# Reordering the first stages of a fused attention and FFN kernel, and 2x2 blocking for half of its last tile

## The chip, the cores and the metric

The kernel runs on one NeuronCore of a Trainium2 chip, in one launch. The metric is device time in microseconds. The five engines that the text speaks of are TensorE (PE, with its weight loads as PEld), VectorE (DVE), ScalarE (ACT), GpSimd (POOL) and SyncE (SP). Each works through its own list of instructions in order and waits at semaphores for the others. Inputs and the output lie in device memory as float32; the kernel computes in bfloat16 with float32 sums.

## The reference

Eight batches of cosFormer attention (8 heads, 576 positions, 64 features per head) feed a multiplicative feed-forward net. Cut to what matters:

```
theta = pi/2 * pos / 576
phi(x) = concat(relu(x)*cos(theta), relu(x)*sin(theta))     # 128 features
kv  = sum over s of phi(k)[s, f] * v[s, d];  z = sum over s of phi(k)
num = phi(q) @ kv;  den = phi(q) @ z + 1e-6
x   = num / den, heads side by side                          # 4608 x 512
a, b = x @ w1, x @ w2                                        # 512 -> 1024
out = ((a * b) @ w3) @ w_out                                 # 1024 -> 1024 -> 512
```

## The kernel before, in words

Attention is done per batch `b` in five chunks `c` of 128 rows (the last of 64). The net is done per tile `t` of 512 tokens, nine tiles in all, so that tile 0 holds rows of batch 0 alone and tile 1 begins with the last 64 rows of batch 0. `w3 @ w_out` is multiplied once into `w34b` (1024 x 512), and every tile then does `(a*b) @ w34b`.

The order of all work is written out by hand in the string `PLAN`; nothing reorders it, and each engine receives its instructions in the order in which the plan's steps issue them. A line of the plan starts with one step `f t` (or `w`, below), which advances tile `t` by one group of matmuls; the other steps of the line come behind it. The steps that the change touches:

- `idle n`: n matmuls of zeros, 128x512, whose result nobody reads (`idle_mms`, L454; tile `unread`).
- `q b c`, `k b c`: the features of a chunk, `x*cos` on DVE (L495) and `x*sin` on ACT (L499) or on DVE (L502). `v b c on`: a copy of `v` into the tile with the column of ones.
- `qt b c on`: eight PE transposes of the q features into the PSUM tile `pst` (two buffers), and a copy into `qpT` by DVE (`V`) or ACT (`A`) (`q_tr`, L567 and L573).
- `kv b`: 40 matmuls (L549) into `pnum`, then the copy `kvs` by ACT (L553) and DVE (L554). For batch 0 this is `kv0`, `ks0`, `kvs0`.
- `n b c`: eight matmuls of a q chunk with `kvs` (L581) into `pnum`. There is one such PSUM tile of two banks in this part of the kernel, so each `n` waits until the last one has been read. For `n 0 0` there is a tile of its own, `pfirst`.
- `d b c`: the division on DVE in three instructions (L592, L593, L594), which reads that PSUM tile and writes `xblk`.
- `xt b c on`: four transposes of `xblk` (L621) and a copy into the tile's `xT` by ACT or DVE (L622).
- `w12`, `wo`, `w3`, `l b name part`: loads, all issued by POOL, in order. A load of `w_out` (`wo a l0 n`) or `w3` (`w3 a g0 n`) covers 32 of the 128 partitions, so four of them make a half of `w_out` or two row blocks of `w3`. `l b k 0` and `l b k 1` are the two parts of a batch's k.
- `t3 jp`: DVE transposes row block `jp` of `w3` into the tile `w3T` (L464), of which there are `NT3` buffers. `w jp lc0 n`: n matmuls (L474) of that block with rows of `w_out`; after the last, ACT copies the sum into `w34b` (L477).
- `open` gives the four PSUM banks of the first part (`ps_first`) to the net's matmuls (`ffn_tile`, four buffers).

In a tile, `f` first makes `a` and `b` (L668): ACT copies `a` out of PSUM and DVE multiplies it with `b` (L711 and L718, L728 and L734, for tiles 0 and 1 also L692 and L694). In tiles 0 and 1 the first groups are cut into quarters of 128 tokens, so that the matmuls of the first 128 tokens can start with one chunk in `xT`. Then comes the product with `w34b`. Tiles 2 to 7 (`SEVEN`) do it as seven products of 256-row blocks with sums and differences on DVE (`seven_products`, `sums`, `weight_block`, L814 and L822). Tiles 0, 1 and 8 do it plainly: for each 128 tokens `ms`, eight matmuls of 512 columns (L749), a copy by ACT (L755) and a store. In tile 8 the last 128 tokens are cut into two halves of 256 columns (L766, L768).

Of the kernel before, what the change touches and what calls it, by code (L numbers as in the profile page):

```python
# [16 lines left out]
P = 128  # L17
# [9 lines left out]
q 0 1; idle 1; idle 1; q 0 0 4; idle 1; idle 1; qt 0 1 V; k 0 4; k 0 1 0; qs 0 3; k 0 0 0; k 0 2; idle 1; k 0 3; qt 0 0 A; ks0 4; idle 3; qc 0 3; ks0 1; kv0 4 0; q 0 2; kv0 1 0; ks0 0; kv0 2 0; kv0 4 1; ks0 3; kv0 0 0; ks0 2; kv0 0 1; kv0 3 0; kvs0 0 A; kv0 1 1; kv0 2 1; kv0 3 1; kvs0 1 V; qt 0 2 A; n0 0; n0 1; idle 1; idle 1; idle 1; w12 0 0 2; w12 1 0 2; w12 0 2 2; n 0 1; idle 2; w12 1 2 2; w12 0 4 2; d 0 0; w12 1 4 2; w12 0 6 2; w12 1 6 2; idle 1; wo 0 0 4; d 0 1; xt 0 0 A; wo 1 0 4; wo 2 0 4; wo 3 0 4; w3 0 0 2; w3 1 0 2; w3 2 0 2; w3 3 0 2; wo 0 4 4; wo 1 4 4; idle 1; qt 0 3 V; wo 2 4 4; wo 3 4 4; w3 0 2 2; w3 1 2 2; w3 2 2 2; w3 3 2 2; w3 0 4 2; w3 1 4 2; w3 2 4 2; w3 3 4 2; q04; w3 0 6 2; xt 0 1 V; w3 1 6 2; open; w3 2 6 2; n 0 2; w3 3 6 2; l 1 q 0; l 1 q 1; l 1 k 0  # L27
f 0; l 1 k 1
f 0; d 0 2; l 1 v 0
f 0; n 0 3; d 0 3; xt 0 2 A  # L30
# [22 lines left out]
w 4 4 4  # L53
# [49 lines left out]
f 2; xd 2 4; xd 3 1  # L103
# [159 lines left out]
NKP, NVA, NQP, NRQ, NRV, NT3 = 1, 2, 1, 2, 2, 3  # L263
# [51 lines left out]
def kernel(  # L315
# [135 lines left out]
    unread = ps_first.tile([P, 512], FP32, name="unread")  # L451
    kva = ps_first.tile([P, 512], FP32, name="kva")

    def idle_mms(n):  # L454

        for _ in range(n):
            nc.tensor.matmul(unread[:, :], lhsT=zeros[:, 0:128], rhs=zeros[:], start=True, stop=True)
# [105 lines left out]
    def q_tr(b, c, on):  # L563
        R = ROWS[c]
        pst = ps_tr.tile([P, 8, 128], BF16, name="pst")
        for h in range(H):
            nc.tensor.transpose(pst[:, h, :], att[b]["qp"][:, c, h, :], identb[:])  # L567
        cols = ds(columns_of(b, c), R)
        if on == "both":
            nc.scalar.copy(out=att[b]["qpT"][:, 0:4, cols], in_=pst[:, 0:4, 0:R])  # L570
            nc.vector.tensor_copy(out=att[b]["qpT"][:, 4:8, cols], in_=pst[:, 4:8, 0:R])
        else:
            on(out=att[b]["qpT"][:, :, cols], in_=pst[:, :, 0:R])  # L573
# [85 lines left out]
    def ffn_groups(t):  # L659
# [39 lines left out]
        seven = t in SEVEN  # L699
        s = [fsb.tile([P, 4, 256], BF16, name=f"s{i}", bufs=1) for i in range(3)] if seven else None  # L700
# [23 lines left out]
        for jc in range(4 if t <= 1 or t in BY_HALF else 0, 8):  # L724
            aT = ffn_tile()
            products(aT[:, :], w1b, jc, slice(0, 512))
            asb = fsb.tile([P, 512], BF16, name="asb")
            nc.scalar.copy(out=asb[:], in_=aT[:, :])  # L728
            newest[0] = asb
            yield  # L730
            bT = ffn_tile()
            products(bT[:, :], w2b, jc, slice(0, 512))
            abT = abT or new_abT()
            nc.vector.tensor_mul(out=abT[:, jc, :], in0=asb[:], in1=bT[:, :])  # L734
# [11 lines left out]
        for ms in range(3 if t == NT - 1 else 4):  # L746
# [14 lines left out]
        if t == NT - 1:  # L761
# [10 lines left out]


# [121 lines left out]
    def num_first(*half):  # L895

        t = att[0]["n"].get(0)
        if t is None:
            t = ps_first.tile([P, 2, 512], FP32, name="pfirst")
        num(0, 0, t, range(4 * half[0], 4 * half[0] + 4) if half else range(H))  # L900
# [3 lines left out]

    V, A, G = nc.vector.tensor_copy, nc.scalar.copy, nc.gpsimd.tensor_copy
# [38 lines left out]
    def store_behind_transposes():  # L944
# [11 lines left out]
        "qt": q_tr, "qh": q_tr_halves, "qd": q_dma, "kv": kv, "kv0": lambda c, *half: kv_first(c, False, *half), "ks0": lambda c: kv_first(c, True), "kvs0": kvs_first,  # L956
# [40 lines left out]
```

## Time and profile before

| | us |
|---|---|
| median of 3 runs (lowest, highest) | 244.58 (243.73, 245.21) |
| the profiled execution | 242.91 |
| its span, from the first to the last instruction | 241.1 |
| PE busy in the span | 234.6 |
| PE busy in the stretch 32 to 48 us | 15.31 of 16.00 |
| PE busy in the stretch 48 to 60 us | 12.00 of 12.00 |
| DVE busy in the stretch 32 to 48 us | 12.95 of 16.00 |
| DMA in the stretch 48 to 60 us | 199 GB/s |

The span leaves out 1.8 us of the execution. In the lists of instructions in order of time a row has the start, the length, the engine, the line, the operation, what it writes and reads with its shape, and how many instructions were merged into it; a bracket at the end tells how long the engine had been idle and whose event ended that. The matmuls of PE overlap: four of 512 columns take 0.86 us from the first start to the next group's start, although the row says 1.03.

### The profile page before, as it was taken

What the parts mean: (1) busy time and instruction counts of PE and PEld (TensorE: products, weight loads), DVE (VectorE), ACT (ScalarE), POOL (GpSimd) and SP (SyncE); (2) the same over time, 40 slices, a digit from 0 to 9 for tenths busy, and PEclk for the clock granted to TensorE, in tenths of its full rate; (3) what the DMA queues carried; (4) which work ended last, traced back from release to release, by engine and by line L of the source; (5) the groups of instructions that cost most, each with busy time, mean ns of one, the idle gap of its engine ahead of it and who ended that gap; (6) DMA issues with size and microseconds to landing.
All of it is one profiled execution on the core that took longest, in us unless ns stands there. A gap on an engine that the chain in (4) does not pass through costs nothing.

```text
span 241.1 us, 5777 instructions
## 1 busy us (share of the span) xinstructions
PE 234.6 (97%) x2227; PEld 162.5 (67%) x2227; DVE 191.9 (80%) x456; ACT 111.9 (46%) x198; POOL 80.0 (33%) x151
## 2 busy tenths in 40 slices
PE   8799989999999999999999999999999999999994
PEld 3589534476964595788579848875995798484442
DVE  6986569968988947999899989999999788786320
ACT  2833321687755832735475437437064312312321
POOL 8744888551803034105402405031020050272000
PEclk9999999999999999999999999999999999999999
DMA  7999999999999999979998987999756936599843
GB/s 200 191 196 199 186 171 186 199 198 197 185 179 137 151 133 182 194 115 163 164 172 105 208 113 107 155 143 136 100 195 129 127 74 157 118 305 312 243 158 130
DMA packets 84939, 40.48 MB, mean 168 GB/s; under 512 B 48048, under 2 KB 82096, under 8 KB 84912
## 3 DMA queue, kind: packets, MB, share of 16 engines
q0 software_dynamic: 37616, 23.60, 65.5%
q1 hardware_dynamic: 47296, 16.52, 39.2%
q8 instruction: 17, 0.28, 0.5%
q14 instruction: 10, 0.08, 0.1%
HBM read 38.80 MB, written 9.44 MB: 200 GB/s over the span
## 4 chain that ended last, share of the span: by engine, by line
PE 84%; DMA 10%; POOL 4%; issue 1%; DVE 1%; DVEq 0%; POOLq 0%
PE ffnps L668 46%; PE ffnps L814 14%; PE ffnps L749 8%; DMA w2b<-in_moe_w_dram 5%; PE ffnps L474 4%; PE pnum L581 4%; PE pnum L549 4%; DMA kf<-in_k_dram 3%; DMA early<-in_moe_w_dram 2%; PE ffnmore L814 1%; PE pst L567 1%; POOL early L407 1%; POOL early L413 1%; PE ffnps L766 1%; POOL w2b L922 1%
## 5 line engine op out<-in xcount | busy, mean ns | idle before, releaser
L668 PE MATMUL ffnps<-xT,w1b 128*128 128x256 bf16 (+2 forms) x448 | 76.3, 303 | 0.0
L668 PE MATMUL ffnps<-xT,w2b 128*128 128x256 bf16 (+2 forms) x448 | 76.2, 303 | 0.0
L668 PEld LDWEIGHTS <-w2b 128*128 128x128 bf16 x448 | 40.7, 98 | 19.6 <-issue 0.2
L668 PEld LDWEIGHTS <-w1b 128*128 128x128 bf16 x448 | 41.0, 98 | 18.8 <-issue 0.4
L728 ACT CAST asb<-ffnps 128x512 bf16<-128x512 f32 x40 | 23.4, 585 | 42.8 <-PE ffnps L668 38.3
L734 DVE TENSOR_TENSOR abT<-asb,ffnps 128x512 bf16<-128x512 bf16 x40 | 27.2, 682 | 14.9 <-PE ffnps L668 14.7
L711 ACT CAST asb<-ffnps 128x512 bf16<-128x512 f32 x24 | 14.1, 586 | 35.6 <-PE ffnps L668 28.5
L594 DVE TENSOR_TENSOR xblk<-pnum,den 128x512 bf16<-128x512 f32 (+1 forms) x39 | 26.9, 691 | 1.3
L499 ACT ACTIVATE kp<-kf,sinv 128x512 bf16<-128x512 bf16 (+4 forms) x33 | 21.0, 662 | 0.9 <-DMA kf<-in_k_dram 0.9
L749 PE MATMUL ffnps<-w34b,abT 128*128 128x512 bf16 x88 | 20.8, 379 | 0.0
L814 PEld LDWEIGHTS <-abT 128*128 128x128 bf16 x192 | 18.5, 98 | 3.1
L718 DVE TENSOR_TENSOR abT<-asb,ffnps 128x512 bf16<-128x512 bf16 x24 | 16.3, 687 | 5.1 <-PE ffnps L668 5.1
L419 POOL COPY seen<-xT 128x1 bf16<-128x1 bf16 x6 | 1.3, 210 | 57.3 <-DMA xT<-xblk 57.3
L499 ACT ACTIVATE qp<-qs,sinv 128x512 bf16<-128x512 bf16 (+6 forms) x30 | 18.1, 626 | 0.9 <-DMA qs<-in_q_dram 0.9
L581 PEld LDWEIGHTS <-qpT 128*128 128x128 bf16 x320 | 15.0, 98 | 4.4 <-DVE qpT L573 0.5
L581 PE MATMUL pnum<-kvs,qpT 128*128 128x65 bf16 x312 | 16.1, 194 | 0.0
L419 POOL COPY seen<-asb 128x1 bf16<-128x1 bf16 x14 | 3.0, 211 | 37.4 <-ACT asb L711 34.8
L474 PE MATMUL ffnps<-early,w3T 128*128 128x512 bf16 x64 | 14.5, 379 | 0.7 <-DVE w3T L464 0.7
L814 PEld LDWEIGHTS <-s 128*128 128x128 bf16 x144 | 14.0, 98 | 1.7
L495 DVE TENSOR_SCALAR kp<-kf,cosv 128x512 bf16<-128x512 bf16 (+1 forms) x40 | 14.8, 392 | 0.1
L749 PEld LDWEIGHTS <-abT 128*128 128x128 bf16 x88 | 8.1, 98 | 8.5
L376 POOL DMA_DIRECT2D vs<-in_v_dram x16 | 12.0, 766 | 2.5 <-DMA kf<-in_k_dram 1.5
(129 smaller groups left out, 341.0 us busy)
## 6 DMA issues: line engine op xcount, KB each, us to landing
out_dram<-osb SPq DMA_DIRECT2D x9, 256.0 KB, 3.4
kf<-in_k_dram POOLq DMA_DIRECT2D x7, 320.0 KB, 6.8
early<-in_moe_w_dram POOLq DMA_DIRECT2D x16, 128.0 KB, 5.1
qs<-in_q_dram POOLq DMA_DIRECT2D x6, 320.0 KB, 6.7
vs<-in_v_dram POOLq DMA_DIRECT2D x6, 320.0 KB, 7.9
kf<-in_k_dram POOLq DMA_DIRECT2D x7, 256.0 KB, 7.1
qs<-in_q_dram POOLq DMA_DIRECT2D x6, 256.0 KB, 7.3
vs<-in_v_dram POOLq DMA_DIRECT2D x6, 256.0 KB, 9.6
```

The source lines that it names most:

```text
L474: nc.tensor.matmul(acc[:, :], lhsT=w3T[:, lc, :], rhs=woutb[:, lc, :], start=(lc == 0), stop=(lc == 7))
L495: nc.vector.tensor_scalar(out=dst[:R, c, :, 0:D], in0=rows[:R], scalar1=0.0, scalar2=cosv[:R, at:at + 1], op0=ALU.max, op1=ALU.mult)
L499: nc.scalar.activation(out=dst[:R, c, 0:n, D:F], in_=rows[:R, 0:n], func=ACTF.Relu, scale=sinv[:R, at:at + 1], bias=0.0)
L581: nc.tensor.matmul(nt[:, h // 4, ds((h % 4) * 65, 65)], lhsT=qpT[:, h, ds(at, 128)], rhs=kvs[:, h, :], start=True, stop=True)
L594: nc.vector.tensor_tensor(out=xblk[rows, g0:g0 + ng], in0=n4[:, :, :, 0:D], in1=den[rows, 0:ng].unsqueeze(3).to_broadcast([R, ng, 4, D]), ...
L668: nc.tensor.matmul(out, lhsT=w[:, kc, ts(jc, 128)], rhs=x[:, kc, tok], start=(kc == 0), stop=(kc == 3))
L711: nc.scalar.copy(out=asb[:], in_=aT[:, :])
L718: nc.vector.tensor_mul(out=abT[:, ts(pair, 2), ts(half, 256)], in0=asb[:].rearrange("p (i n) -> p i n", i=2), in1=bT[:, :].rearrange("p (i ...
L728: nc.scalar.copy(out=asb[:], in_=aT[:, :])
L734: nc.vector.tensor_mul(out=abT[:, jc, :], in0=asb[:], in1=bT[:, :])
L749: nc.tensor.matmul(ops[:, :], lhsT=abT[:, jc, ts(ms, 128)], rhs=w34b[:, jc, :], start=(jc == 0), stop=(jc == 7))
L814: nc.tensor.matmul(into[:, ts(ms, 256)], lhsT=a[:, kc, ts(ms, 128)], rhs=b[:, kc, :], start=(ms == 0 and kc == 0), stop=(ms == 1 and kc == 3))
```

## The change

It has two parts. The first is in the plan, up to tile 1:

- four of the seven `idle` matmuls between the first `n` and the first `f 0` go, and three stay. In their place stand `qt 0 3`, copied by halves (the new step `qy`: half 0 by ACT, half 1 by DVE), and the matmuls of `n 0 2`, which write a new PSUM tile `spare` (step `ns`). `spare` takes the place of `unread` and `kva`: its first bank is the target of `idle` and of `ns`, its second is `kva`. Two of the three `idle` write `pfirst`.
- `f 0` starts before `xt 0 1`; `xt 0 1` and `n 0 3` follow its first group, and `d 0 2` and `d 0 3` come ahead of tile 0's first products on DVE.
- POOL loads `w3` row blocks 2 and 3 ahead of the second half of `w_out`. `w` runs the first four row blocks by halves: `w 0 0 4` to `w 3 0 4`, then `w 0 4 4` to `w 3 4 4`; `t3 2`, `t3 3`, `t3 4` and `t3 6` are done by halves, and `w3T` has four buffers.
- `kv 1` moves behind the next group of `f 0`. `k 2 4` and `k 2 2`, which stood behind `d 1 4`, now stand ahead of it; between `n 1 4` and `n 1 0` there is one group of `f 0` where there were two.
- `xd 3 1` and `xd 2 4` change places.

The second part is in tile 8: its first 256 tokens go through seven products of blocks of 128 rows and 256 columns (`small_products`), the sums of the left blocks being made by DVE in the loop over `jc`, the sums of the results by DVE and POOL. The last 256 tokens are done as before.

```
-... n0 0; n0 1; idle 1; idle 1; idle 1; w12 ...; n 0 1; idle 2; w12 ...; d 0 0; w12 ...; idle 1; wo 0 0 4; d 0 1; xt 0 0 A; wo 1 0 4; wo 2 0 4; wo 3 0 4; w3 0 0 2; w3 1 0 2; w3 2 0 2; w3 3 0 2; wo 0 4 4; wo 1 4 4; idle 1; qt 0 3 V; wo 2 4 4; wo 3 4 4; w3 0 2 2; w3 1 2 2; w3 2 2 2; w3 3 2 2; w3 0 4 2; ... q04; w3 0 6 2; xt 0 1 V; w3 1 6 2; open; w3 2 6 2; n 0 2; w3 3 6 2; l 1 q 0; l 1 q 1; l 1 k 0
-f 0; l 1 k 1
-f 0; d 0 2; l 1 v 0
-f 0; n 0 3; d 0 3; xt 0 2 A
+... n0 0; n0 1; qt 0 3 N; w12 ...; n 0 1; idle 1; ns 0 2; w12 ...; d 0 0; w12 ...; wo 0 0 4; d 0 1; qy 0 3 0 A; xt 0 0 A; wo 1 0 4; wo 2 0 4; wo 3 0 4; w3 0 0 2; w3 1 0 2; w3 2 0 2; w3 3 0 2; w3 0 2 2; w3 1 2 2; w3 2 2 2; w3 3 2 2; wo 0 4 4; wo 1 4 4; idle1 2; qy 0 3 1 V; d 0 2; wo 2 4 4; wo 3 4 4; w3 0 4 2; ... q04; w3 0 6 2; w3 1 6 2; open; w3 2 6 2; w3 3 6 2; l 1 q 0; l 1 q 1; l 1 k 0
+f 0; xt 0 1 A; n 0 3; l 1 k 1
+f 0; d 0 3; l 1 v 0
+f 0; xt 0 2 A
...
-f 0; lg 2 q 0; t3 1; l 2 k 0; l 2 k 1; l 2 q 1; t3 2; l 2 v 0
+f 0; lg 2 q 0; t3 1; l 2 k 0; l 2 k 1; l 2 q 1; l 2 v 0
 f 0
-f 0
+f 0; t3 2 0 4; t3 3 0 4; t3 2 4 4; t3 3 4 4
 w 0 0 4
-w 0 4 4
 w 1 0 4
-w 1 4 4
-w 2 0 4; t3 3; t3 4
-w 2 4 4; q 0 4 0
+w 2 0 4
 w 3 0 4
-w 3 4 4; t3 5; qt 0 4 V; t3 6
-w 4 0 4; n 0 4; t3 7; d 0 4
-w 4 4 4
+w 0 4 4; t3 4 0 4; t3 4 4 4
+w 1 4 4; q 0 4 0
+w 2 4 4
+w 3 4 4; t3 5
+w 4 0 4; qt 0 4 V; t3 6 0 4; t3 6 4 4
+w 4 4 4; n 0 4; t3 7; d 0 4
...
 f 0; qt 1 4 A; qt 1 2 A; l 3 q 0; v 2 2 G; v 1 0 V; v 1 1 V
-f 0; qt 1 0 A; v 1 2 V; v 1 3 V; kv 1
-f 0; qt 1 1 A; n 1 4; d 1 4; k 2 4; k 2 2 2
-f 0
+f 0; qt 1 0 A; v 1 2 V; v 1 3 V
+f 0; kv 1; qt 1 1 A; k 2 4; k 2 2 2
+f 0; n 1 4; d 1 4
 f 0; n 1 0; d 1 0; xt 1 4 A; q 2 0 0; q 2 1; lt 3 v 0; xt 0 4 A
...
-NKP, NVA, NQP, NRQ, NRV, NT3 = 1, 2, 1, 2, 2, 3
+NKP, NVA, NQP, NRQ, NRV, NT3 = 1, 2, 1, 2, 2, 4
...
-    unread = ps_first.tile([P, 512], FP32, name="unread")
-    kva = ps_first.tile([P, 512], FP32, name="kva")
+    pfirst = ps_first.tile([P, 2, 512], FP32, name="pfirst")
+    spare = ps_first.tile([P, 2, 512], FP32, name="spare")
+    kva = spare[:, 1, :]
...
-        seven = t in SEVEN
+        seven, small = t in SEVEN, t == NT - 1
...
-        for ms in range(3 if t == NT - 1 else 4):
+        if small:
+            yield from small_products(t, abT, s)
+        for ms in (2,) if small else range(4):
...
+    def small_products(t, abT, s):
+
+        s3, s2, s4 = (x[:, :, 0:128] for x in s)
+        t1, t2, t3, t4 = blocks
+        osb = osb_of(2 * t)
+        c11, c12, c21, c22 = (osb[:, r, ts(c, 256)] for r in range(2) for c in range(2))
+        a11, a12, a21, a22 = (A_small(abT, r, c) for r in range(2) for c in range(2))
+        b11, b21, b22 = B_of(0, 0), B_of(1, 0), B_of(1, 1)
...
+            for kc in range(4):
+                nc.tensor.matmul(bank[:, 0:256], lhsT=a[:, kc, :], rhs=b[:, kc, :], start=(kc == 0), stop=(kc == 3))
...
+        nc.scalar.copy(out=c11, in_=product(a11, b11))
+        nc.scalar.copy(out=c22, in_=product(s3, t3, True))
+        yield
+        m2 = product(a12, b21)
+        add(c21, product(s2, t2), c11)
+        yield
+        add(c12, product(a21, t1, True), c21)
+        add(c21, c21, c22, nc.gpsimd)
+        add(c11, m2, c11)
+        add(c22, c22, c12, nc.gpsimd)
+        yield
+        add(c21, product(a22, t4), c21)
+        store(nc.sync, osb[:, 1:2, :], 4 * t + 1, 1)
+        add(c12, product(s4, b22), c12)
+        store(nc.sync, osb[:, 0:1, :], 4 * t, 1)
+        yield
```

More of the change, by code (lines that the diff above doesn't have):

```diff
@@ L567, in q_tr, with q_copy @@
             nc.tensor.transpose(pst[:, h, :], att[b]["qp"][:, c, h, :], identb[:])
[L568 to L571, printed above, removed]
-        else:
-            on(out=att[b]["qpT"][:, :, cols], in_=pst[:, :, 0:R])
+        if on is None:
+            uncopied[b, c] = pst
+        else:
+            on(out=att[b]["qpT"][:, :, ds(columns_of(b, c), R)], in_=pst[:, :, 0:R])
+    uncopied = {}
+    def q_copy(b, c, half, on):
+        on(out=att[b]["qpT"][:, ts(half, 4), ds(columns_of(b, c), ROWS[c])],
+           in_=uncopied[b, c][:, ts(half, 4), 0:ROWS[c]])
     def num(b, c, tile=None, heads=range(H)):
@@ L895, in num_first @@
     def num_first(*half):
[L897 to L900, printed above, removed]
+        num(0, 0, pfirst, range(4 * half[0], 4 * half[0] + 4) if half else range(H))
     def kvs_first(i, on):
         on(out=att[0]["kvs"][:, 4 * i:4 * i + 4, :], in_=att[0]["halves"][i][:, 0:260])
+    N = None
     V, A, G = nc.vector.tensor_copy, nc.scalar.copy, nc.gpsimd.tensor_copy
```

47 lines of the change are left out of this document (29 added, 18 removed).

## The prediction

> **What bounds the kernel now.** I read first the page's head and the table of busy time by stretches, to see which engine has no idle time.
>
> ```profile
> span 241.1 us, 5777 instructions
> PE 234.6 (97%) x2227; PEld 162.5 (67%) x2227; DVE 191.9 (80%) x456; ACT 111.9 (46%) x198; POOL 80.0 (33%) x151
> ...
> 32.00:48.00 16.00, 15.31 (x83) 6.85 (x82) 12.95 (x25) 6.13 (x12) 11.94 (x20) 1.00 1.41 188
> 48.00:60.00 12.00, 12.00 (x165) 8.37 (x163) 9.00 (x29) 9.60 (x18) 3.92 (x4) 1.00 1.44 199
> 60.00:205.00 145.00, 144.98 (x1480) 109.58 (x1477) 129.82 (x314) 71.98 (x132) 34.62 (x70) 1.00 1.03 147
> ```
>
> Each row gives a stretch, its length, the busy time of PE, PEld, DVE, ACT and POOL, the granted clock, the DMA share and GB/s. From 60 to 205 us PE is busy for 144.98 of 145 us, at the full clock (1.00). So a microsecond that PE loses before 60 us is lost at the end too, and one that it gains arrives only if nothing on the way holds PE back. Next I read PE, DVE and ACT in order of time for the stretches that the diff touches. At the start:
>
> ```profile
> 13.81 0.81 PE L457 MATMUL unread<-zeros 128*128 128x512 bf16 x3
> 14.72 0.81 PE L457 MATMUL unread<-zeros 128*128 128x512 bf16 x3
> 15.59 0.38 PE L457 MATMUL unread<-zeros 128*128 128x512 bf16 x1
> 16.90 0.39 PE L668 MATMUL ffnps<-xT,w1b 128*128 128x128 bf16 x4
> 19.17 1.04 PE L668 MATMUL ffnps<-xT,w1b 128*128 128x256 bf16 x8
> ...
> 15.48 0.69 DVE L594 TENSOR_TENSOR xblk<-pnum,den 128x512 bf16<-128x512 f32 x1
> 17.06 0.41 DVE L622 COPY xT<-pst 128x512 bf16<-128x512 bf16 x1
> 17.39 0.15 DVE L592 TENSOR_SCALAR den<-pnum 128x8 f32<-128x8 f32 x1
> 17.82 0.69 DVE L594 TENSOR_TENSOR xblk<-pnum,den 128x512 bf16<-128x512 f32 x1
> ...
> 60.06 0.45 PE pst L567 x8
> 55.24 0.26 PE pnum L581 x8
> ```
>
> Seven zero products fill PE while DVE divides; the last two rows, of the chain that ended last, price eight transposes and eight matmuls of `n`. A division takes from 17.39 to 18.51, 1.12 us; `d 0 1` ends at 16.17. Then the stage of `w34b`:
>
> ```profile
> 31.80 3.62 PE L474 MATMUL ffnps<-early,w3T 128*128 128x512 bf16 x16
> 36.11 3.63 PE L474 MATMUL ffnps<-early,w3T 128*128 128x512 bf16 x16 [0.69 <-DVE w3T L464]
> ...
> 34.81 1.25 DVE L464 STREAM_TRANSPOSE w3T<-early 128x1024 bf16<-128x1024 bf16 x1 [2.35 <-DMA early<-in_moe_w_dram]
> ```
>
> Here is the one real hole: DVE waits for the load of `w3` blocks 2 and 3 until 34.81, and PE for DVE. Matmuls of 512 columns start 0.216 us apart (the tail's row below: 24 in 5.18), so sixteen end their starts at 35.25, and the next start at 36.11: 0.86 us.
>
> **The change part by part.**
>
> *The start.* PE loses four zero products (0.86 us) and gains work that stood later: eight transposes (0.45) and eight matmuls of `n` (0.26). But the net's first two groups of PSUM lie where `pfirst` and `spare` lay, and as built the first `w2` group of `f 0` waits for the end of `d 0 2`, which reads `spare`. On DVE that is 16.17, plus a half copy of `qpT` less the overlap (0.41 for as many elements, L622: about 16.5), plus 1.12: 17.6. Before, that group was 0.23 behind 16.90. Then follow, on PE, `xt 0 1` 0.22, `n 0 3` 0.26, a group of 0.45, a wait for ACT's copy of `xT` of some 0.15, four quarters 0.9 and `xt 0 2` 0.22: the row at 19.17 moves to about 20.0, 0.8 to 0.9 late. That is a loss, and tile 0 carries it to the stage of `w34b`, which starts at about 32.65.
>
> *The loads.* Nothing is added: on POOL's queue four `wo` loads change places with four `w3` loads, so blocks 2 and 3 are on hand four transfers sooner, and the second half of `w_out` lands by about 34.7, where those landed. `w 2 0 4` wants to start at 34.4, and its transposed half is ready at about 34.3 behind four operations of DVE. The hole of 0.86 goes; the late start of 0.85 uses it up. `t3 4` and later blocks wait for the same landings as before. PE ends the stage about 0.2 us sooner than before (47.2). The four halves add four instructions on DVE where it would wait for loads: nothing. The fourth `w3T` buffer costs no time.
>
> *The pinch at batch 1.* This decides the sum.
>
> ```profile
> 47.44 1.03 PE L749 MATMUL ffnps<-w34b,abT 128*128 128x512 bf16 x4
> 53.09 0.42 PE L581 MATMUL pnum<-kvs,qpT 128*128 128x65 bf16 x8
> 53.35 1.89 PE L749 MATMUL ffnps<-w34b,abT 128*128 128x512 bf16 x8
> 55.08 0.42 PE L581 MATMUL pnum<-kvs,qpT 128*128 128x65 bf16 x8
> 58.74 0.39 PE L668 MATMUL ffnps<-xT,w1b 128*128 128x128 bf16 x4
> ...
> 54.58 0.81 DVE L495 TENSOR_SCALAR kp<-kf,cosv 64x512 bf16<-64x512 bf16 x2
> 55.30 0.32 DVE L502 TENSOR_SCALAR kp<-kf,sinv 128x384 bf16<-128x384 bf16 x1
> 55.53 0.17 DVE L592 TENSOR_SCALAR den<-pnum 128x8 f32<-128x8 f32 x1
> 55.97 0.69 DVE L594 TENSOR_TENSOR xblk<-pnum,den 128x512 bf16<-128x512 f32 x1
> ...
> 55.09 0.40 ACT L499 ACTIVATE kp<-kf,sinv 128x128 bf16<-128x128 bf16 x1 [0.17 <-DMA kf<-in_k_dram]
> ...
> 43.00 1.37 POOL L376 DMA_DIRECT2D kf<-in_k_dram  x2 [1.60 <-DVE w3T L464]
> ...
> kf<-in_k_dram POOLq DMA_DIRECT2D x1, 256.0 KB, 11.3
> ```
>
> Before, `n 1 4` (53.09) is divided at once, two groups of matmuls hide that, and `n 1 0` starts at 55.08. `k 2 4` and `k 2 2` run behind the division. In the changed order DVE does those two first, and `k 2 2` needs the second part of batch 2's k. That was issued at 43.7 and landed 11.3 us later, at 55.0; ACT's row shows the same moment. The order and the bytes of the loads ahead of it are the same, and DMA runs at 199 GB/s there, so it lands at 55.0 again. Then the DVE rows from 55.30 on repeat with `d 1 4` in `d 1 0`'s place: it ends at 56.66. There is one PSUM tile for `n`, so `n 1 0` starts at 56.72. PE, 0.2 us ahead of before up to there (`kv 1` behind a group of 0.86 makes `n 1 4` start at 53.75), would be ready at 54.87: a stall of 1.85 us. Against 55.08, everything from `n 1 0` on is 1.64 us late. Behind it the order is as before; `n 1 1` waits for `d 1 0`, hidden by two groups (1.73 against 1.12 plus some 0.45 to begin), so tile 1 starts at 60.35 for 58.74. Cost: +1.6 us. Because PE has 1.85 us to spare ahead of the pinch, the first two parts count nothing at the end.
>
> *Tile 8.*
>
> ```profile
> 213.55 0.87 PE ffnmore L814 x8
> 230.85 5.18 PE ffnps L749 x24
> ...
> 230.96 0.69 DVE L734 TENSOR_TENSOR abT<-asb,ffnps 128x512 bf16<-128x512 bf16 x1 [1.04 <-PE ffnps L668]
> 237.82 0.42 DVE L768 COPY osb<-ffnps 128x256 f32<-128x256 f32 x1 [6.17 <-PE ffnps L766]
> ...
> 60.84 0.62 POOL L514 COPY va<-vs 128x512 bf16<-128x512 bf16 x1
> ```
>
> Sixteen matmuls of 512 columns (16 x 0.216 = 3.45 us) become 28 of 256 (28 x 0.109 = 3.05): -0.41 us. The left sums that need DVE's last product (ends 231.65) are wanted 1.5 us after the stage's start at 230.7, later than they are ready (some 232.1). DVE's five sums of results (0.42 each by the copy's row) and POOL's two run beside the 3.5 us of the last 256 tokens. POOL has no such sum before; nearest is its copy, 0.62. The last PSUM bank is wanted at 236.35, and POOL's first sum can start at 233.6, so anything from 0 to 2.3 us is free. The two stores now leave at about 234.7 and 235.2, ahead of the rest; the last store keeps its distance to PE's end.
>
> *Sum.* +1.6 - 0.4 = +1.2 us: 242.9 becomes 244.1 in a profiled execution. The median of the runs shown is 1.67 above that execution, so 245.8, which is +0.5%. About 0.5% is what a measurement of this kernel can tell from no change. Ends: with k landing in time, DVE's order alone still ends `d 1 4` at about 55.3 (two features of 0.9 in all, then 1.12, from `kvs` at 53.3), so the pinch costs at least 0.25; with the landing 0.5 later, 2.1.
>
> **The clock.**
>
> ```profile
> 235.87 1.91 PE L766 MATMUL ffnps<-w34b,abT 128*128 128x256 bf16 x16
> 239.80:240.00 0.20, 0.00 (x0) 0.00 (x0) 0.00 (x0) 0.00 (x0) 0.00 (x0) 0.88 0.00 0
> ...
> 1.20 6.07 PE L457 MATMUL unread<-zeros 128*128 128x512 bf16 x20 [1.20 <-DVE zeros L434]
> ```
>
> PE ends at 237.78, and the granted clock falls at about 239.95, 2.2 us later; the new stall is 1.85. Twenty zero products at the start take 6.07 us where the full rate gives 4.3: a slow start costs about 1.75. If the stall shuts the clock, that comes on top.
>
> The Trainium skill, "TensorE: Matmul & The Clock Gate", Part 1, says that the clock falls back after at least one idle window of about 3.4 us. By that rule the stall is too short and the sum stays 245.8; the trace's fall after 2.2 us bears it out only in part, because its window may have held the last matmuls. The same page, Part 4, says transposes do not count as activity like other matmuls; that speaks against putting them for zero products, and a slow clock in tile 0 would be taken up by the pinch but for some 0.3 us by my rows.
>
> **Rivals.** *The clock shuts in the stall*: 245.8 + 1.75 = 247.5. For it: 1.85 is near 2.2; against: PE idles 0.7 us at most elsewhere, so no row shows a shorter fall. Chance 0.2. *Not slower: k lands earlier.* If reordered loads are moved faster, each microsecond that it lands before 55.0 gives one back; from 1.2 us earlier (53.8) the kernel is no slower, and the floor is 0.25 - 0.4, so 244.4. For it: DMA ran at 188 GB/s from 32 to 48 us, under its 199; against: the same bytes by the same issues. Chance 0.15. *A larger wait*: the landing slips by 0.5, or tile 8's chain of sums shows: 246.3. Chance 0.1.
>
> **How the numbers follow.** The forecast has 0.55, and lies on the 0.5% line, so half of it counts as slower, half as no change. Slower: 0.2 + 0.1 + 0.27 = 0.57. Same: 0.28 + 0.1 = 0.38. Faster by over 0.5% needs something that I don't see: 0.05, taken from the early landing. The range goes from 244.4 (early landing) to 247.5 (the clock), with 0.2 at either end for the spread of runs.
>
> **What would show it.** PE idle for about 1.9 us ahead of L581 near 56.7, released by DVE; no hole in L474; L668's first group split by a wait near 17; tile 1 about 1.6 us late; tile 8's products ending 0.4 us nearer to its start. Wrong if `n 1 0` starts before 55.5, or if the hole in L474 stays.

## The result and the profile after

The changed kernel takes 246.79 us, the median of 19 runs (244.48 to 250.05), against 243.78 us for the kernel before on the same chip (19 runs, 241.85 to 246.41): a ratio of 1.011, with a 95% interval of 1.0081 to 1.0138. Run a second time beside the last experiments it took 245.77 us against 243.30, a ratio of 1.0094 (1.0059 to 1.0129). It is about 1% slower. Every ratio in this text leaves out the executions that lie more than 1.5% above the fastest of their kernel, three of the changed kernel's 19 and in one experiment (transposes_late) seven of twelve. The forecast had the sign, and the time lies in its range, but the step of +1.2 us came out as +2.5 to +3.0 us.

The profiled execution of the changed kernel lasted 247.63 us, 4.7 us more than the profiled one of before (242.91). The page of after: its head, PE's busy row, and the shares of the chain that ended last.

```profile
span 245.9 us, 5819 instructions
PE 234.7 (95%) x2235; PEld 163.4 (66%) x2235; DVE 194.7 (79%) x470; ACT 112.4 (46%) x200; POOL 81.0 (33%) x153
...
PE 67%; DMA 18%; DVE 8%; POOL 4%; issue 2%; ACT 0%; DVEq 0%; POOLq 0%
```

PE is as long busy as before (234.7 for 234.6 us) in a span that is 4.8 us longer. So nothing new is computed that costs; PE waits. Of the chain that ended last DMA has 18% where it had 10% before, and DVE 8% where it had 1%. The table of stretches of after says where (stretch, length, busy time of PE, PEld, DVE, ACT and POOL, granted clock, DMA share, GB/s):

```profile
17.00:32.00 15.00, 13.75 (x142) 10.27 (x142) 8.23 (x18) 5.40 (x10) 8.76 (x16) 1.00 1.33 183
32.00:48.00 16.00, 16.00 (x89) 7.63 (x88) 12.57 (x23) 5.39 (x10) 11.30 (x19) 1.00 1.38 185
48.00:60.00 12.00, 9.61 (x121) 6.03 (x120) 7.88 (x29) 8.58 (x16) 4.32 (x4) 1.00 1.40 199
60.00:90.00 30.00, 29.80 (x344) 20.22 (x342) 25.84 (x70) 18.75 (x36) 8.54 (x17) 1.00 1.14 139
```

The stage of `w34b` (32 to 48) has lost its hole: 16.00 of 16 us. The start (17 to 32) lost 1.25 us, where PE was busy for 15.00 of 15.00 us before, and the stretch around batch 1 (48 to 60) lost 2.39 of 12 us, where before had none. The clock stays at 1.00. The rows of those places, from the same execution in order of time:

```profile
17.28 0.38 PE L673 MATMUL ffnps<-xT,w1b 128*128 128x128 bf16 x4 [0.24 <-ACT xT L627]
18.61 0.38 PE L673 MATMUL ffnps<-xT,w2b 128*128 128x128 bf16 x4 [0.94 <-DVE xblk L599]
21.00 1.04 PE L673 MATMUL ffnps<-xT,w1b 128*128 128x256 bf16 x8
33.64 7.93 PE L475 MATMUL ffnps<-early,w3T 128*128 128x512 bf16 x36
51.44 0.38 PE L756 MATMUL ffnps<-w34b,abT 128*128 128x512 bf16 x1 [0.50 <-ACT w34b L478]
55.81 0.42 PE L586 MATMUL pnum<-kvs,qpT 128*128 128x65 bf16 x8
58.82 0.43 PE L586 MATMUL pnum<-kvs,qpT 128*128 128x65 bf16 x8 [1.73 <-DVE xblk L599]
...
57.17 0.35 DVE L496 TENSOR_SCALAR kp<-kf,cosv 128x512 bf16<-128x512 bf16 x1 [0.98 <-DMA kf<-in_k_dram]
57.44 0.32 DVE L503 TENSOR_SCALAR kp<-kf,sinv 128x384 bf16<-128x384 bf16 x1
58.08 0.68 DVE L599 TENSOR_TENSOR xblk<-pnum,den 64x512 bf16<-64x512 f32 x1
...
45.10 1.36 POOL L376 DMA_DIRECT2D kf<-in_k_dram  x2 [0.85 <-DVE w3T L465]
```

Read from below: POOL issues the two parts of batch 2's k; DVE's `k 2 2` waits for the second until 57.17; the division `d 1 4` (58.08) stands behind it; PE's `n 1 0` (58.82) waits 1.73 us for that division. At 51.44 there is a smaller one that I had not foreseen, 0.50 us for the last copy of `w34b` on ACT. Above it: the wait for `d 0 2` at 18.61, and 36 matmuls in one piece at 33.64, where before had two pieces with a hole between them.

`n 1 0` starts at 58.82 for 55.08, +3.74 us, more than the 1.64 foreseen. In this execution the group at 21.00 (the first one of pair 1, at 19.17 before) is 1.83 us late instead of 0.85, and k was issued 2.1 us later than before and again took 11.3 us. In the second profile of the same kernel, shown with the last experiments, `n 1 0` starts at 56.32. Where `n 1 0` lies also varies without any change ahead of it: in the profiles of the kernels below that have the kernel before's plan up to there it starts at 55.39, 55.46 and 56.78. So a difference of a microsecond between two profiles says little; the waits and their releasers say more. Behind `n 1 0` something is lost as well, and at the end too. Both are taken apart below.

### The profile page after: what moved, and what is told of

Its sections match the earlier page's. It is cut to its first block, busy times and chain, and to the rows that moved or that the text cites. A ratio compares the mean times of both kernels' runs of the same rounds, so it can differ in the third digit from the quotient of the medians.

```text
span 245.9 us, 5819 instructions
## 1 busy us (share of the span) xinstructions
PE 234.7 (95%) x2235; PEld 163.4 (66%) x2235; DVE 194.7 (79%) x470; ACT 112.4 (46%) x200; POOL 81.0 (33%) x153
## 4 chain that ended last, share of the span: by engine, by line
PE 67%; DMA 18%; DVE 8%; POOL 4%; issue 2%; ACT 0%; DVEq 0%; POOLq 0%
PE ffnps L673 44%; PE ffnps L864 11%; DMA kf<-in_k_dram 8%; DMA early<-in_moe_w_dram 5%; DMA w2b<-in_moe_w_dram 4%; PE pnum L550 3%; PE pnum L586 3%; POOL early L407 2%; PE ffnps L756 2%; PE ffnmore L864 1%; DVE xblk L599 1%; DVE kp L496 1%; PE ffnps L797 1%; DVE qp L496 1%; DVE q0f L872 1%
## 5 line engine op out<-in xcount | busy, mean ns | idle before, releaser
L599 DVE TENSOR_TENSOR xblk<-pnum,den 128x512 bf16<-128x512 f32 (+1 forms) x38 | 26.3, 691 | 1.3
L864 PEld LDWEIGHTS <-abT 128*128 128x128 bf16 x192 | 18.5, 98 | 3.2
L756 PE MATMUL ffnps<-w34b,abT 128*128 128x512 bf16 x72 | 17.7, 379 | 0.5 <-ACT w34b L478 0.5
L496 DVE TENSOR_SCALAR qp<-qs,cosv 128x512 bf16<-128x512 bf16 (+1 forms) x35 | 13.0, 382 | 0.0
```

Of the source, the lines that this page charges most:

```text
L496: nc.vector.tensor_scalar(out=dst[:R, c, :, 0:D], in0=rows[:R], scalar1=0.0, scalar2=cosv[:R, at:at + 1], op0=ALU.max, op1=ALU.mult)
L599: nc.vector.tensor_tensor(out=xblk[rows, g0:g0 + ng], in0=n4[:, :, :, 0:D], in1=den[rows, 0:ng].unsqueeze(3).to_broadcast([R, ng, 4, D]), ...
L756: nc.tensor.matmul(ops[:, :], lhsT=abT[:, jc, ts(ms, 128)], rhs=w34b[:, jc, :], start=(jc == 0), stop=(jc == 7))
L864: nc.tensor.matmul(into[:, ts(ms, 256)], lhsT=a[:, kc, ts(ms, 128)], rhs=b[:, kc, :], start=(ms == 0 and kc == 0), stop=(ms == 1 and kc == 3))
```

## The experiments

In every diff, lines with - are of the kernel that was edited, and a row of the plan is cut to the steps that moved. All ratios are to the kernel before in the same runs.

### The parts apart: batch 1 put back, and batch 1 alone

The changed kernel with the kernel before's order of batch 1, and the reverse:

```diff
 # undo_batch1: from the changed kernel (batch1_alone: the same, reversed, in the kernel before)
-f 0; qt 1 0 A; v 1 2 V; v 1 3 V
-f 0; kv 1; qt 1 1 A; k 2 4; k 2 2 2
-f 0; n 1 4; d 1 4
+f 0; qt 1 0 A; v 1 2 V; v 1 3 V; kv 1
+f 0; qt 1 1 A; n 1 4; d 1 4; k 2 4; k 2 2 2
+f 0
```

> The changed kernel with the batch 1 steps in the order of before (kv 1 one group sooner, d 1 4 ahead of k 2 4 and k 2 2, two groups between n 1 4 and n 1 0). Pinch theory: n 1 0 no longer waits for the division (under 0.3 us idle ahead of it, where the changed kernel has 1.73), and the time falls 1.6 us or more below the changed kernel's, to 0.2 to 0.6 us below before. Rival, the reordered loads: the w3 loads in a row move batch 1's and 2's loads later by about 1 us, whatever the order of the steps; then this kernel is still about 1 us slower than before, and the second part of batch 2's k lands after 56.

> The kernel before with the batch 1 steps of the changed one alone. Pinch theory: PE idles about 1.7 us ahead of n 1 0 for DVE's division, which stands behind the feature of batch 2's k that waits for its landing at 55; slower than before by 1.2 to 1.7 us. Rival, the loads: no change, since the loads are those of before.

Measured: 243.21 us without the change at batch 1, ratio 0.9986 (0.9951 to 1.002), and 245.80 us with it alone, ratio 1.0041 (1.0004 to 1.0078). Without these three lines nothing is lost that the runs can tell. Alone they cost 0.4%, less than the 1.1% of the whole change (1.0081 to 1.0138), though the interval reaches that of its second run (1.0059 to 1.0129); so it isn't shown that they make up the whole loss without the rest of the change. In order of time, batch 1's part alone:

```profile
56.72 0.43 PE L581 MATMUL pnum<-kvs,qpT 128*128 128x65 bf16 x8 [1.77 <-DVE xblk L594]
97.95 0.43 PE L581 MATMUL pnum<-kvs,qpT 128*128 128x65 bf16 x8 [1.87 <-DMA qpT<-qp]
...
55.07 0.35 DVE L495 TENSOR_SCALAR kp<-kf,cosv 128x512 bf16<-128x512 bf16 x1 [1.18 <-DMA kf<-in_k_dram]
72.20 0.29 DVE L514 COPY va<-vs 128x512 bf16<-128x512 bf16 x1 [1.02 <-DMA vs<-in_v_dram]
```

The first row is the step as forecast, to the hundredth: k lands at 55.07, and `n 1 0` starts at 56.72, 1.64 us late. But the span is 245.6, 4.5 us over that of before (this execution took 247.35 us, 1.55 above the median of its kernel). The other two rows are waits that the kernel before doesn't have: DVE for batch 3's v at 72.20, and PE for a transposed q at 97.95. That the order behind the pinch (the tight place at batch 1) stays as it was is not enough for it to cost nothing.

### The load order alone, and tile 8 alone

```diff
 # loads_alone: the kernel before with
-w3 3 0 2; wo 0 4 4; wo 1 4 4; ...; wo 2 4 4; wo 3 4 4; w3 0 2 2; w3 1 2 2; w3 2 2 2; w3 3 2 2
+w3 3 0 2; w3 0 2 2; w3 1 2 2; w3 2 2 2; w3 3 2 2; wo 0 4 4; wo 1 4 4; ...; wo 2 4 4; wo 3 4 4
 # ... the w34b stage by halves as in the changed kernel, and NT3 = 4
 # small_alone: the plan of before with tile 8's seven products (small_products); helpers and
 # PSUM tiles are those of the changed kernel
```

> The kernel before with the order of the w3 and w_out loads, the products by halves and the four transposed buffers alone. Pinch theory: the hole of 0.86 us in the w34b products goes, PE waits at most 0.3 us there, batch 2's k lands at 55 as before; 0.2 to 0.7 us faster. Rival, the loads: the hole goes too, but batch 2's k lands about 1 us later (56 or after), and the gain is taken back: within 0.3 us of before, or slower.

> The kernel before with the seven products in tile 8 alone. Both theories: the stage from the first product with w34b to DVE's last copy takes 0.4 us less than before (6.97 in the trace of before), no wait of PE in it; 0.4 us faster, which the runs may not tell from no change.

Measured: 243.99 us, ratio 1.0000 (0.9959 to 1.0042), and 243.77 us, ratio 0.9996 (0.9955 to 1.0036). The load order does what was forecast: the hole goes, `n 1 0` starts at 54.69 instead of 55.08, and batch 2's k is not delayed (11.3 us, as before). Yet the 0.2 to 0.7 us that were expected of it don't show in the time. Tile 8 is no gain either, though PE's stage is 0.4 us shorter; the section on the end says why.

### The front alone, and two parts together

```diff
 # front_alone: the kernel before with the change's first four plan lines, its helpers and banks,
 # but the load order, the w34b stage, batch 1 and tile 8 of before
 # loads_and_small: loads_alone and small_alone together
```

> The kernel before with the front of the change alone: steps of batch 0 in the place of six of seven zero products, the second pair of banks and its wait for d 0 2, copies of q by halves; load order, w34b stage, batch 1 and tile 8 as before. Theory (as predicted): the pair-1 group starts 0.8 to 0.9 us later than 19.17, the w34b stage too, and the 0.86 us hole in it closes, so that n 1 0 starts within 0.4 us of where it does in the kernel before; ratio 0.998 to 1.002. Rival (the lateness of the front is not taken up by the hole): n 1 0 about 0.9 us later, ratio 1.003 to 1.005.

> The kernel before with two parts of the change: the load order with its w34b stage by halves, and tile 8's seven products; front and batch 1 as before. Theory (the parts add): the hole of 0.86 us closes, n 1 0 starts 0.2 to 0.4 us earlier, tile 8's stage is 0.4 us shorter; ratio 0.996 to 0.999, some 0.6 us under the kernel before. Rival (what the first part brings goes in waits behind it): ratio 0.998 to 1.001, with tile 8's 0.4 us alone or nothing.

Measured: front_alone 243.52 us, ratio 1.0007 (0.9975 to 1.0039); its pair-1 group starts at 19.84, 0.67 us late. loads_and_small 243.94 us, ratio 1.0016 (0.9986 to 1.0046), no gain, so the rival is the nearer. The lateness of the front was not taken up quite as I put it, for `n 1 0` starts at 56.14, 1.06 us late, yet the time doesn't tell it from no change, and another profile has `n 1 0` as late without any change to the front (56.78 in small_alone).

### The order on DVE alone

The changed kernel with two steps put back behind the division; `n 1 4` and `d 1 4` stay one group later:

```diff
-f 0; kv 1; qt 1 1 A; k 2 4; k 2 2 2
-f 0; n 1 4; d 1 4
+f 0; kv 1; qt 1 1 A
+f 0; n 1 4; d 1 4; k 2 4; k 2 2 2
```

> The changed kernel with one thing put back: on DVE the features of batch 2's k (k 2 4, k 2 2) stand behind the division d 1 4 again; n 1 4, d 1 4 stay one group later. Theory now: the features ahead of the division cost twice. Once at n 1 0 (its wait was 1.73 us in the changed kernel's profile), and again at 60 to 68 us, because batch 2's transposes of q, late by the stall, then run beside batch 3's loads of v, q and k, which landed 9.6 to 11 us after their issue instead of 6 to 7.5, so that DVE waited 1.0 to 1.3 us for v at 72 to 75 us. If that is so, both go together here: the wait ahead of n 1 0 falls to at most 0.5 us, those loads land in 6 to 7.5 us, DVE has no wait for v, and the ratio to the kernel before is 0.999 to 1.003. Rival 1 (only the stall itself hangs on the order, the later losses do not): the wait shrinks, the loads still land in 9 to 11 us, ratio 1.004 to 1.007. Rival 2 (the later group for n 1 4 or the front is what costs): ratio stays at 1.008 to 1.013.

Measured: 244.10 us, ratio 1.0019 (0.9994 to 1.0044), 0.7 to 0.9% less than the changed kernel. Two rows of it, the wait at `n 1 0` and the stretch behind it:

```profile
55.48 0.43 PE L586 MATMUL pnum<-kvs,qpT 128*128 128x65 bf16 x8 [0.34 <-DVE xblk L599]
```

```profile
60.00:90.00 30.00, 30.00 (x344) 21.60 (x342) 24.73 (x65) 18.21 (x35) 10.36 (x20) 1.00 1.13 152
```

The wait falls to 0.34 us (`n 1 0` is 0.40 us later than before), and from 60 to 90 us PE never waits. Batch 3's v of 256 KB lands after 6.6 us, and DVE doesn't wait for it. The order of two features and a division on DVE is the cause of both losses, the one at `n 1 0` and the one behind it. Rivals 1 and 2 fall.

### What is lost behind the pinch

At 57 to 61 us SP issues the DMA transposes of batch 2's q, as soon as DVE has the features; they stand behind `d 1 0` and so come later by the stall. POOL issues batch 3's loads of q, v and k, which follow a landing and not DVE. So the distance between the two shrinks. First I moved the features by one group in the kernel before:

```diff
 # late_q2
-f 0; n 1 0; d 1 0; xt 1 4 A; q 2 0 0; q 2 1; lt 3 v 0; xt 0 4 A
-f 0; v 2 0 G
+f 0; n 1 0; d 1 0; xt 1 4 A; lt 3 v 0; xt 0 4 A
+f 0; v 2 0 G; q 2 0 0; q 2 1
```

> The kernel before with one thing moved: the features of batch 2's first two q blocks (q 2 0, q 2 1) stand one group later on DVE and ACT, so that their transposes through the DMA queue are issued some 1 to 2 us later, next to batch 3's loads of v and q; nothing waits at n 1 0. Theory (transposes that run beside the loads stretch the loads): no wait ahead of n 1 0, yet batch 3's v, q and k land 9 to 11 us after their issue instead of 6 to 7, DVE waits about 1 us for v at some 70 us, and the ratio is 1.002 to 1.008. Rival (the slow landings after 60 us come from the run, or from the stall and not from the neighbourhood): the loads land in 6 to 7.5 us, no wait for v, ratio 0.998 to 1.002.

Measured: 243.61 us, ratio 1.0020 (0.9989 to 1.0050), inconclusive: between the two places DVE has nothing else to do, and the transposes were issued at 57.60 instead of 57.29. The edit didn't move what it was to move. The next one put the features behind a division, and another held the loads back in the changed kernel; beside them the changed kernel ran unaltered:

```diff
 # transposes_late: the kernel before with
-f 0; n 1 0; d 1 0; xt 1 4 A; q 2 0 0; q 2 1; lt 3 v 0; xt 0 4 A
+f 0; n 1 0; d 1 0; xt 1 4 A; lt 3 v 0; xt 0 4 A
-f 1; lg 3 q 1; d 1 1; qd 2 0; n 1 2; ...
+f 1; lg 3 q 1; d 1 1; q 2 0 0; q 2 1; qd 2 0; n 1 2; ...
 # loads_held: the changed kernel with
-f 0; n 1 0; d 1 0; xt 1 4 A; q 2 0 0; q 2 1; lt 3 v 0; xt 0 4 A
+f 0; n 1 0; d 1 0; xt 1 4 A; q 2 0 0; q 2 1; xt 0 4 A
-f 1; lg 3 q 1; d 1 1; qd 2 0; n 1 2; ...
+f 1; d 1 1; qd 2 0; lt 3 v 0; l 3 q 1; n 1 2; ...
```

> The kernel before with one thing moved: the features of batch 2's first two q blocks (q 2 0, q 2 1) stand behind the division d 1 1 on DVE, so that their transposes are issued at about 59.8 us instead of 57.29 us, some 0.3 us ahead of batch 3's first load of v (60.16 us) instead of 2.9 us; nothing waits at n 1 0. Theory (transposes that run beside the loads stretch the loads): no wait ahead of n 1 0, yet batch 3's v, q and k land 9 to 11 us after their issue instead of 6 to 7, DVE waits about 1 us for v near 70 us, ratio 1.002 to 1.008. Rival (the slow landings hang on something else that the stall brings): the loads land in 6 to 7.5 us, no wait for v, ratio 0.998 to 1.002.

> The changed kernel with batch 3's loads of v and q held until the first transpose of batch 2's q has landed, so that they are issued at 66 to 67 us and later instead of 62.08 us. The wait ahead of n 1 0 stays (1.5 to 1.8 us). Theory (neighbourhood): held, the loads land 6 to 7.5 us after their issue, where they took 7.4 to 10 in the changed kernel, so that issuing 4 to 5 us later costs at most 2.5 us in landing, and DVE's wait for v changes by less than 1.5 us; ratio 1.006 to 1.016. Rival (the loads are slow whatever runs beside them): they land 9 to 11 us after issue, at 76 us and later, DVE's wait for v is 3 to 5 us, ratio over 1.014.

> The changed kernel once more, unaltered, for a second profile of it and its time beside the others. Theory (the order on DVE costs twice): wait of 1.5 to 1.9 us ahead of n 1 0, batch 3's loads of v, q and k landing 9 to 11 us after issue, DVE waiting about 1 us for v; ratio 1.006 to 1.013. What may differ, if it belonged to the run: the 1.0 us by which the first load of k was late in the first profile, and the 11.3 us that the second part of batch 2's k took. Rival (the cost is the stall alone): ratio 1.003 to 1.006.

Measured: transposes_late 248.27 us (243.66 to 254.49), ratio 1.0072 (1.0021 to 1.0122); loads_held 245.93 us, ratio 1.0128 (1.0076 to 1.0179); the changed kernel again (after_again) 245.77 us, ratio 1.0094 (1.0059 to 1.0129). Whether the wide spread of transposes_late is its own doing is open. In loads_held the first load was issued at 62.49 us and not at 66 to 67 as expected, since the transposes landed sooner there. The next five fences, each of one kernel, show the DMA issues from 59.5 to 66 us (destination and source, queue, operation and count, KB each, us from issue to landing). The kernel before:

```profile
qs<-in_q_dram POOLq DMA_DIRECT2D x1, 256.0 KB, 6.0
vs<-in_v_dram POOLq DMA_DIRECT2D x1, 256.0 KB, 5.8
```

Batch 1's part alone:

```profile
qs<-in_q_dram POOLq DMA_DIRECT2D x1, 256.0 KB, 9.7
vs<-in_v_dram POOLq DMA_DIRECT2D x1, 256.0 KB, 9.7
```

The kernel before with late transposes:

```profile
qs<-in_q_dram POOLq DMA_DIRECT2D x1, 256.0 KB, 9.1
vs<-in_v_dram POOLq DMA_DIRECT2D x1, 256.0 KB, 9.5
qpT<-qp SPq DMA_TRANSPOSE x2, 9.3
```

The changed kernel with the loads held:

```profile
qs<-in_q_dram POOLq DMA_DIRECT2D x1, 256.0 KB, 6.0
vs<-in_v_dram POOLq DMA_DIRECT2D x1, 256.0 KB, 6.1
qpT<-qp SPq DMA_TRANSPOSE x2, 3.3
```

The changed kernel again:

```profile
qs<-in_q_dram POOLq DMA_DIRECT2D x1, 256.0 KB, 8.8
vs<-in_v_dram POOLq DMA_DIRECT2D x1, 256.0 KB, 8.9
```

The same 256 KB land 6 us after their issue or 9 to 10 us, and it goes by how long ahead the transposes were issued. From the issue rows of SP and POOL in the profiles (us; after is the first profile of the changed kernel, after_again the second; the last column is the time from issue to landing of the 256 KB of v, the second part of that load):

| kernel | transposes issued | first load of v issued | distance | landing |
|---|---|---|---|---|
| loads_held | 58.42 | 62.49 | 4.07 | 6.1 |
| before | 57.29 | 60.16 | 2.87 | 5.8 |
| k2_behind | 57.84 | 60.14 | 2.30 | 6.6 |
| small_alone | 58.99 | 61.06 | 2.07 | 6.9 |
| undo_batch1 | 58.76 | 60.50 | 1.74 | 6.4 |
| after_again | 58.54 | 59.77 | 1.23 | 8.9 |
| after | 61.04 | 62.08 | 1.04 | 9.8 |
| batch1_alone | 58.94 | 59.78 | 0.84 | 9.7 |
| transposes_late | 60.80 | 59.84 | -0.96 | 9.5 |

The other profiles agree (front_alone, late_q2, loads_alone, loads_and_small and row2_first): at a distance of 2.3 to 2.7 us that v takes 6.0 to 6.6 us.

The DMA queues from 62 to 68 us show what happens there (queue, packets, MB, the time that they took); q0 carries POOL's loads, q1 SP's transposes. The kernel before, then batch 1's part alone:

```profile
q0 software_dynamic: 1784, 0.98, 120.5%
q1 hardware_dynamic: 559, 0.14, 10.7%
```

```profile
q0 software_dynamic: 922, 0.53, 77.4%
q1 hardware_dynamic: 1056, 0.26, 43.7%
```

Where the transposes are nearly through by 62 us, the loads move 0.98 MB in 6 us; where they run beside them, 0.53 MB. The kernel with late transposes has no stall at `n 1 0` (55.46) and shows it all the same, and it pays in PE's time, by waits at two places, the second of them behind an instruction by which POOL waits for a transposed q:

```profile
63.69 0.43 PE L581 MATMUL pnum<-kvs,qpT 128*128 128x65 bf16 x8 [1.04 <-DVE qpT L573]
71.28 1.18 PE L549 MATMUL pnum<-va,kp 128*128 128x65 bf16 x32 [2.05 <-POOL va L514]
...
69.42 0.34 POOL L419 COPY seen<-qpT 128x1 bf16<-128x1 bf16 x1 [6.27 <-DMA qpT<-qp]
```

The first of these waits is not the neighbourhood's: DVE's copy of `qpT` stands behind the moved features. The second is so at least in part: the transpose was issued 3.5 us later than in the kernel before and took 8.5 us instead of 5.0. POOL waits 6.27 us for it, and its copy of `va` stands behind that wait.

So the neighbourhood theory holds for the landings, with the stall at `n 1 0` (loads_held has 1.27 us of it and fast landings) and without. Held back, the loads were issued 2.1 to 2.7 us later than in after_again, and the v of 256 KB landed at 70.5 us (64.40 + 6.1) instead of 71.3 (62.35 + 8.9). It doesn't account for the whole of the lost time. With the loads held DVE no longer waits for v, yet the kernel is no faster, and PE's last copy is still 0.7 us later than `n 1 0` and tile 8 explain (+1.41 us at the last copy, +1.12 at `n 1 0`, and 0.40 gained in tile 8). The next transpose (69.10 us) took 8.1 us to land there, beside k's load. What part of the lost time goes back to the slow landings therefore stays open.

The second profile of the changed kernel in order of time, and its table of stretches:

```profile
21.04 1.04 PE L673 MATMUL ffnps<-xT,w1b 128*128 128x256 bf16 x8
54.70 0.42 PE L586 MATMUL pnum<-kvs,qpT 128*128 128x65 bf16 x8
56.32 0.43 PE L586 MATMUL pnum<-kvs,qpT 128*128 128x65 bf16 x8 [0.34 <-DVE xblk L599]
95.99 0.43 PE L586 MATMUL pnum<-kvs,qpT 128*128 128x65 bf16 x8 [0.73 <-DMA qpT<-qp]
```

```profile
13.00:15.00 2.00, 2.00 (x31) 2.00 (x29) 0.55 (x3) 0.87 (x2) 1.22 (x3) 0.50 1.45 197
```

Here the wait ahead of `n 1 0` is 0.34 us, against an expectation of 1.5 to 1.9: the start was 1.87 us late (21.04 for 19.17), in this execution with the clock at half for some 3 us, so `n 1 4` itself came at 54.70, when k had landed. `n 1 0` starts at 56.32 all the same, 1.24 us late, but here by the late front and not by the order on DVE: k2_behind, with the old order, has the same wait of 0.34 us. A late front and the wait at the pinch don't add; the later of the two counts, as the prediction had it. Another 0.87 us are lost behind (last copy 239.53 for 237.82, +1.71; +1.24 at `n 1 0`, and 0.40 gained in tile 8). That loss goes with the order: undo_batch1 has in its profile a front as late by the same slow clock (20.95) and `n 1 0` at 56.54, and loses nothing behind it (last copy 238.86). Most of the loss behind is idle time of PE in front of a transposed q near 96 to 98 us, 0.73 us here and 1.87 us with batch 1's part alone, which neither undo_batch1 nor k2_behind has; in the first profile of the changed kernel that wait is missing, and only 0.4 of its 0.99 us can be seen as idle time of PE.

### The end

SP's issues of tile 8's output, in order of time, in the kernel before (whose last copy on DVE, at 237.82, stands in the prediction) and, with DVE's last copy, in the changed one; and below each the landing of the stores, from the DMA issues of the same executions.

```profile
233.23 5.37 SPq L653 DMA_DIRECT2D out_dram<-osb  x5
```

```profile
out_dram<-osb SPq DMA_DIRECT2D x3, 256.0 KB, 2.4
out_dram<-osb SPq DMA_DIRECT2D x2, 128.0 KB, 2.0
```

```profile
240.07 2.86 SPq L658 DMA_DIRECT2D out_dram<-osb  x5
242.15 0.42 DVE L775 COPY osb<-ffnps 128x256 f32<-128x256 f32 x1 [1.64 <-PE ffnps L773]
```

```profile
out_dram<-osb SPq DMA_DIRECT2D x3, 256.0 KB, 2.7
out_dram<-osb SPq DMA_DIRECT2D x2, 128.0 KB, 2.7
```

Before, four row blocks of the output leave over 5.4 us; with seven products two of them become ready only at the end of the products, and all leave within 2.9 us. The two stores of 128 KB, which are the last, land 2.7 us after issue in the median instead of 2.0, and the very last of them 2.3 instead of 1.9. From the start of DVE's last copy to the end of the span it is 3.3 us in the kernels without the seven products (241.1 - 237.82 before, 240.8 - 237.49 with the load order alone) and 3.75 to 3.9 with them (245.9 - 242.15; 241.6 - 237.84 in k2_behind; 242.7 - 238.88 with tile 8 alone). The other profiles lie in these two groups (3.3 to 3.4 us and 3.75 to 3.9). The DMA engines fit that: from 0.5 to 1.5 us behind the start of the last copy their busy share is 0.6 and 0.4 in the two halves before, and 0.98 and 0.99 in the changed kernel, so the last stores go while the engines are still full. PE's 0.4 us are given back by the stores; that it is by their standing together is the reading, and the last run was to test it by turning tile 8 round:

```diff
 # row2_first: loads_and_small with
-        if small:
-            yield from small_products(t, abT, s)
         for ms in (2,) if small else range(4):
             ...
+        if small:
+            yield from small_products(t, abT, s)
```

> The kernel before with the load order, the w34b stage by halves and tile 8's seven products, and within tile 8 one thing turned round: its third row block is computed and stored ahead of the seven products instead of behind them. Theory (tile 8's 0.40 us of PE work are given back at the end, because all four row blocks are stored within 2.9 us there instead of 5.4 us, and the last one lands 3.8 us after DVE's last copy instead of 3.3 us): with one row block out of the way the end comes 3.3 to 3.6 us after the last copy, PE's tile 8 stays 0.4 us shorter than in the kernel before, ratio 0.997 to 1.001. Rival (the longer end does not come from the stores standing together): the end stays at 3.7 to 3.9 us after the last copy, ratio 0.999 to 1.004.

Measured: 244.54 us, ratio 1.0052 (1.0016 to 1.0087), slower, and outside both expectations. PE is again 0.4 us sooner through (last copy at 237.27), but the end comes 4.8 us after it (242.1 - 237.27):

```profile
out_dram<-osb SPq DMA_DIRECT2D x3, 256.0 KB, 2.4
out_dram<-osb SPq DMA_DIRECT2D x2, 128.0 KB, 2.9
```

The third row block is indeed out of the way, but the two row blocks of the products moved right up to the last one, so more bytes stand together at the very end, and the two stores of 128 KB take 2.9 us. SP issues the last of them at 238.32, 1.05 us behind the start of DVE's last copy instead of 0.45, as it had three others to issue from 237.0 on. It was the wrong way to turn them. It agrees with the reading that stores standing together are what costs, but doesn't show it: a turn that spreads them was not tried.

No version beats the kernel before by more than can be told: the fastest, undo_batch1, has 0.9986 (0.9951 to 1.002).

## Why the prediction was right in sign and short in size

*The start*: right. 0.8 to 0.9 us late were forecast; with the clock at full speed the first group of pair 1 starts 0.67 (front_alone), 0.81 (loads_held) and 1.03 us (k2_behind) late, by the wait for `d 0 2` that was named. The first profile's 1.83 has a late load of k in it, the second's 1.87 a slow clock.

*The loads*: right. No hole, and with the load order alone k takes the same 11.3 us to land; the rival that reordered loads move k's landing falls. The term was put at nothing for the end, and alone it brings nothing that the runs can tell.

*The pinch*: right in mechanism and, in its own run, in size: 56.72 foreseen and measured with batch 1's part alone. That it came out to the hundredth is luck: in the three profiles with the whole change up to there `n 1 0` starts at 56.20 to 58.82, as the features of k could start at 54.6 (loads_held) to 57.2; "it lands at 55.0 again" was the part that varied from one execution to the next. In the second profile k lands ahead of `n 1 4`, and `n 1 0` waits for the division no longer than in k2_behind (0.34 us).

*"Behind it the order is as before"* is the step that failed. It took all that follows `n 1 0` for a plain shift. Transposes of q follow DVE and loads of batch 3 follow a landing, so the stall pushes the one onto the other, and the loads take 3 to 4 us longer to land. From `n 1 0` to the last copy the changed kernel lost 0.99 and 0.87 us more, tile 8's gain apart, batch 1's part alone 2.77 us, and k2_behind 0.02. That the order on DVE brings this loss is shown; that it comes by the slow landings is shown in part only, as with the loads held 0.7 us of it remained.

*Tile 8*: the 0.41 us of PE were right (0.40 in the first profile: the stage takes 6.57 us to the last copy instead of 6.97), and PE had no wait. "The last store keeps its distance to PE's end" was wrong: from the start of DVE's last copy to the end it grew from 3.3 to 3.8 us, and the term is +0.1 instead of -0.4.

*The clock rival* didn't come: with PE idle for 1.73 us at `n 1 0`, and 2.05 us in the kernel with late transposes, the granted clock stayed at 1.00, as the stretch of 48 to 60 us above shows for the one and this stretch of the other:

```profile
60.00:90.00 30.00, 26.91 (x313) 18.49 (x311) 23.53 (x66) 17.53 (x34) 8.29 (x16) 1.00 1.16 143
```

The Trainium skill, "TensorE: Matmul & The Clock Gate", Part 1, which lets the clock fall only after an idle window of about 3.4 us, agrees with these two rows. In the tails the fall came sooner than the Trainium skill has it, 2.2 us behind PE's last matmul in the kernel before and 2.9 us in k2_behind, so what a stall a little longer than these does stays open. The rival's price of 1.75 us had no support: the profile gives a granted clock of 1.00 from 1.2 to 7.2 us too. Over whole executions the mean granted clock is 0.993 or less in 16 of 30 of the changed kernel and in 6 of 109 of the kernel before; where it fell, only the second profile shows (near 12 to 16 us, below). It isn't what makes the change slower, for the other 14 executions take 245.7 us in the mean, and those of the kernel before 243.7.

In sum, by the second profile: +1.24 at `n 1 0` (here by the late front), +0.87 behind it, -0.40 in tile 8 and +0.6 at the stores, which is the +2.3 us of its span (243.4 for 241.1). The forecast of 245.8 us is near the 245.77 of the second run (246.79 in the first) in part by luck: it stood on 244.58 us for the kernel before, which ran in 243.30 beside it.

## What to carry to other kernels

When a stall is costed, list the transfers on both sides of it and ask what each follows: those that follow the stalled engine move, those that follow a landing don't, and where they met here the loads got slower. An operation with a late input must not stand in an in-order queue ahead of a short one that the busiest engine waits for. A saving on the last tile has to be costed to the landing of the last store: here the stores gave it back.

## What the runs showed of the hardware

DMA transposes through SP's queue slowed plain loads through POOL's by more than their bytes tell. Transposes issued 1.74 us or more ahead of the loads left them at 5.8 to 6.9 us for 256 KB; issued 1.23 us ahead or later they made it 8.9 to 9.8 us, in fourteen profiles. The transposes themselves took 3.3 us with the loads held back and 9.3 us in transposes_late; in the other profiles 4.6 to 5.9 us (the middle of the two), whether the loads beside them were fast or slow. The Trainium skill, "Advanced Engine Details and Errata", X-Bar Transpose (TRN2), says that transpose DMAs are as fast as regular ones; here both queues together moved 0.79 MB from 62 to 68 us, by the two rows above, against 1.12 MB in the kernel before. The Trainium skill may be right for transposes alone; of company it says nothing, and by what means the loads are slowed no run here shows.

In two of the profiles (after_again and undo_batch1) the granted clock stood at half for some 3 us near 12 to 16 us, while PE was busy throughout (2.00 of 2.00 us in the row above). What triggers it stays open.
